# Running the first group alone through a two-block pipeline, and moving a weight conversion from GpSimd to VectorE and ScalarE

## The chip, the cores and the metric

The kernel runs on one core of one Trainium2 chip. The time is the device time of one execution in microseconds (us), and the lower the better. A core has five engines with their own instruction queues, each of which runs in order: TensorE (PE, matrix products and transposes), VectorE (DVE), ScalarE (ACT), GpSimd (POOL), and SyncE (SP), which issues most of the loads here. They wait for each other through semaphores. TensorE's clock is throttled: the profile records at which share of full speed it was let run, and here that share is 1.0 or 0.5.

Before the change the median was 373.23 us of three runs (372.49 to 373.57).

## The reference

Two blocks, one after the other, in fp32; the weights `w_in` and `w_out` arrive in fp64.

```python
# q, k, v, alpha: (B, H, S, D) = (4, 8, 768, 48)
for t in range(S):                                  # gated linear attention
    state = alpha[:, :, t, :, None] * state + einsum('bhd,bhe->bhde', k[:, :, t], v[:, :, t])
    y[:, :, t] = einsum('bhd,bhde->bhe', q[:, :, t], state)
x = y.transpose(0, 2, 1, 3).reshape(B, S, 384)

proj = x @ w_in                                     # w_in (384, 1024)
val, gate = proj[..., :512], proj[..., 512:]
a = exp(A_log)
for t in range(S):                                  # the SSM block
    h = a * h + val[:, t, :]
    ys[:, t, :] = h
return (silu(gate) * ys) @ w_out                    # w_out (512, 384)
```

## The kernel before

The 4 x 768 steps are cut into 12 groups of 256 steps, three to a batch. A group passes through three Python generators, and every call of `step(...)` emits one piece of one generator's instructions. A hand-written loop calls them in the order in which the engines are to receive the work.

- `front(n)`: alpha is transposed and scanned to running products V (backwards) and P (forwards); then Q, K, the 64-step blocks of scores, masked to A, and the transposed keys Kn. Two ScalarE passes over V (`junk`, L311 and L313) check that its values stay in range; the prediction calls them the checks.
- `back(n)`: the state at the start of each block (S_n), the outputs from inside the blocks (`y`, L145) and from the states before them (L163), and their transpose xT.
- `ssm(n)`: the SSM block. Four times a projection `pj`, a scan `hh`, `sg = silu`, and their product `f`; then twice an output product `o`.

```python
    def ssm(n, xT, prev_h, pool, ps_mm):
        ...
        for cc in range(NI):                                     # NI = 4
            pj = ps_mm.tile([C, 2, GC], FP32, tag="mm", name="pj")
            for i in range(2):
                for kk in range(NK):                             # NK = 3
                    nc.tensor.matmul(pj[:, i, :], w_in[:, kk, i, ds(cc * C, C)], xT[:, kk, :], ...)
            ...  # hh: scan on VectorE (L96)
            nc.scalar.activation(sg, pj[:, 1, :], AF.Silu)       # L101
            nc.vector.tensor_mul(f[:, cc, :], sg, hh)            # L102
            yield
        for c in range(G):                                       # G = 2
            ...  # o: NI matmuls of f with w_out (L107), copied out by ScalarE, stored
            yield
```

The fp64 weights are turned into fp32 by integer work on their two 32-bit words: eight units of `w_in` and four of `w_out`, each of 128 x 384 numbers. This is the unit as it was:

```python
        def split_unit(u):
            lo, hi = words[u][..., 0], words[u][..., 1]
            dst = units[u][0]
            nc.scalar.activation(lo.bitcast(FP32), lo, AF.Copy, scale=2.0 ** -52)
            ex = ...
            nc.vector.tensor_scalar(out=ex, in0=hi, ...)                 # exponent   (L235)
            nc.vector.tensor_scalar(out=dst.bitcast(U32), in0=hi, ...)   # mantissa   (L237)
            nc.scalar.activation(dst, dst.bitcast(U32), AF.Copy, scale=2.0 ** -20)
            nc.gpsimd.tensor_scalar(out=ex, in0=ex, ... ALU.max, ALU.min)  # clamp    (L240)
            nc.gpsimd.tensor_scalar(out=ex, in0=ex, ... ALU.add, ALU.mult) # rebias   (L241)

        def join_unit(u):
            nc.vector.scalar_tensor_tensor(out=ex, in0=hi, ...)          # sign       (L247)
            nc.gpsimd.tensor_add(dst, dst, lo.bitcast(FP32))             # low word   (L249)
            nc.gpsimd.tensor_mul(dst, dst, ex.bitcast(FP32))             # scale      (L250)
```

The state product also stood on GpSimd:

```python
            if not first:                                                # first group of a batch
                nc.gpsimd.tensor_mul(S_n[:, 0], S_end[0], s["V"][:, :, 0:1].to_broadcast([C, NP, D]))  # L347
            zv = block_states(s["Kn"], v_sb, ps_y)                       # z
            for x in range(GR):                                          # GR = 4
                ...  # nc.vector.tensor_add: S_n of the next block, or S_end   (L354, L356)
```

The loop runs three groups at once from the start. `front(n)`, `back(n - 1)`, the projections of `n - 2` (`new`) and the output products of `n - 3` (`old`) share turn n, and the weight conversion (`turn`) is fed in during turns 0 to 2:

```python
            for n in range(N + 3):
                fr, ba = front(n), back(n - 1)                           # where they exist
                old, new = ssms[n - 3], None
                turn = weights if n < 3 else None
                step(fr); step(turn); step(ba); step(old); step(old)
                step(fr); step(turn); step(ba)
                new = ssms[n - 2] = ssm(n - 2, ...)
                step(new); step(fr)
                ...                                                      # loads of n + 2
                step(turn); step(ba); step(new); step(fr); step(ba)
                step(turn); step(new); step(fr); step(turn); step(new)
```

## Time and profile before

| | before |
|---|---|
| time, median of 3 | 373.23 us |
| span of the profiled execution | 372.8 us |
| TensorE busy | 325.8 us, 87% |
| VectorE busy | 200.5 us, 54% |
| GpSimd busy | 56.8 us, 15% |
| mean granted TensorE clock | 0.975 |

A landmark that every turn has makes the timeline easy to cut: the first V scan of each group. I write V(n) for the moment at which it starts. Before, V(0) to V(4) are at 8.21, 30.85, 53.96, 89.22 and 115.25 us. The differences are 22.64, 23.11, 35.26 and 26.03 us, and from then on a turn takes 26.04 to 26.42 us. (Taken from the timeline, such a start lies 0.1 us or less before the one the chain of waits gives for the same scan, because the two views draw the edge differently.) The profile's lines are shown in the prediction below.

### The profile page before, as it was taken

To read this page: it belongs to the slowest core of one execution; us is meant where nothing else is said; L and a number is where in the kernel's file an instruction comes from. 1 tells how busy PE (TensorE), PEld (TensorE's weight loads), DVE (VectorE), ACT (ScalarE), POOL (GpSimd) and SP (SyncE) were. 2 spreads that over 40 slices of the span, in tenths; PEclk is the share of its full clock that TensorE was granted. 3 is DMA by queue.
4 is the path that set the end of the run, shared out by engine and by line. 5 is a ranking of instruction groups with operands and counts; after the bars stand their busy time and mean duration, and the time that the engine had idled before them with its cause. 6 is when DMAs were issued, how large, how long until landed. Compare 5 with 4: busy or idle time off the path is not lost.

```text
span 372.8 us, 9626 instructions
## 1 busy us (share of the span) xinstructions
PE 325.8 (87%) x4233; PEld 265.6 (71%) x4233; DVE 200.5 (54%) x373; ACT 106.5 (29%) x231; POOL 56.8 (15%) x77
## 2 busy tenths in 40 slices
PE   2535851899999999999999999999999999999794
PEld 1425741787887886887887887878868868878582
DVE  3939785356557438348456555565484493403140
ACT  1414354221432323133223213223332231312111
POOL 4478898510000000000000000000000000000000
PEclk9999995599999999999999999999999999999999
DMA  9999992040470740911913704607401000010101
GB/s 132 212 220 190 303 171 47 2 86 2 105 111 2 154 60 3 179 36 41 145 30 80 134 2 100 115 3 130 85 2 44 2 16 30 2 45 0 38 7 50
DMA packets 107650, 29.02 MB, mean 78 GB/s; under 512 B 100944, under 2 KB 107088, under 8 KB 107600
## 3 DMA queue, kind: packets, MB, share of 16 engines
q1 hardware_dynamic: 104992, 27.93, 40.6%
q10 hardware_dynamic: 2608, 0.40, 0.9%
q8 instruction: 35, 0.57, 0.7%
q14 instruction: 15, 0.12, 0.1%
HBM read 23.60 MB, written 4.72 MB: 76 GB/s over the span
## 4 chain that ended last, share of the span: by engine, by line
PE 62%; DVE 23%; SPq 6%; issue 4%; POOL 2%; DMA 1%; ACT 1%; ACTq 0%; DVEq 0%; POOLq 0%
PE pj L93 35%; PE y L145 7%; DVE V L301 7%; DVE P L306 7%; PE o L107 4%; SPq L83 4%; PE y L163 4%; PE sc L331 3%; PE tp L294 3%; DVE S_n L356 3%; PE tpk L119 2%; PE tpx L172 2%; SPq L226 2%; DVE hh L96 2%; DMA bits<-in_moe_w_in_dram 1%
## 5 line engine op out<-in xcount | busy, mean ns | idle before, releaser
L93 PE MATMUL pj<-xT,w_in 128*128 128x256 f32 x576 | 136.1, 388 | 0.0
L93 PEld LDWEIGHTS pj<-xT,w_in 128*128 128x128 f32 x576 | 107.7, 193 | 14.6
L96 DVE TENSOR_TENSOR_SCAN hh<-a_dec,hh,pj 128x256 f32<-128x256 f32 x32 | 23.9, 747 | 78.2 <-PE pj L93 78.2
L107 PE MATMUL o<-w_out,f 128*128 128x384 f32 x192 | 65.0, 492 | 0.0
L101 ACT ACTIVATE sg<-pj 128x256 f32<-128x256 f32 x48 | 18.4, 383 | 130.9 <-DVE hh L96 130.9
L107 PEld LDWEIGHTS o<-w_out,f 128*128 128x128 f32 x192 | 35.5, 190 | 23.0 <-DVE f L102 0.5
L145 PE MATMUL y<-v_sb,A 64*64 64x48 f32 x768 | 28.0, 233 | 11.9 <-DVE S_end L356 11.2
L347 POOL TENSOR_TENSOR S_n<-S_end,V 128x192 f32<-128x192 f32 x8 | 4.1, 513 | 224.2 <-DVE S_end L356 224.2
L145 PEld LDWEIGHTS y<-v_sb,A 64*64 64x64 f32 x768 | 26.7, 149 | 15.1 <-issue 8.3
L306 DVE TENSOR_TENSOR_SCAN P<-tp,iV,bias 128x256 f32<-128x256 f32 x48 | 33.4, 738 | 0.8
L102 DVE TENSOR_TENSOR f<-sg,hh 128x256 f32<-128x256 f32 x48 | 20.4, 426 | 23.3 <-ACT sg L101 23.3
L301 DVE TENSOR_TENSOR_SCAN V<-tp,bias 128x256 f32<-128x256 f32 x48 | 30.1, 669 | 5.1 <-PE tp L294 5.1
L96 DVE TENSOR_TENSOR_SCAN hh<-a_dec,pj 128x256 f32<-128x256 f32 x16 | 11.0, 687 | 39.4 <-PE pj L93 39.4
L311 ACT ACTIVATE junk<-V,bias 128x1024 f32<-128x1024 f32 x12 | 13.8, 1148 | 52.7 <-DVE V L301 52.7
L294 PE MATMUL tp<-ident,a_pad 128*128 128x128 f32 x96 | 14.6, 300 | 15.6 <-POOL ex L240 7.2
L294 PE MATMUL tp<-ident,q_pad 128*128 128x128 f32 x96 | 15.5, 306 | 11.9 <-DVE P L306 7.7
L294 PEld LDWEIGHTS tp<-ident,a_pad 128*128 128x128 f32 x96 | 12.4, 154 | 17.4 <-POOL ex L240 7.5
L294 PEld LDWEIGHTS tp<-ident,q_pad 128*128 128x128 f32 x96 | 12.4, 157 | 16.4 <-issue 13.8
L240 POOL TENSOR_SCALAR ex<-ex 128x384 uint32<-128x384 uint32 x12 | 18.4, 1532 | 18.0 <-DVE ex L235 17.7
L331 PEld LDWEIGHTS sc<-Q,K 64*64 64x64 f32 x768 | 13.7, 144 | 4.3 <-issue 3.3
L334 DVE COPY_PREDICATED A<-mask,sc 128x512 f32<-128x512 uint8 x24 | 16.0, 721 | 1.1 <-PE sc L331 1.1
L322 DVE TENSOR_TENSOR K<-tp,V 128x512 f32<-128x512 f32 x24 | 15.5, 684 | 2.0 <-PE tp L294 2.0
(59 smaller groups left out, 315.6 us busy)
## 6 DMA issues: line engine op xcount, KB each, us to landing
a_pad<-in_alpha_dram SPq DMA_DIRECT2D x24, 192.0 KB, 4.7
k_pad<-in_k_dram SPq DMA_DIRECT2D x24, 192.0 KB, 5.1
v_sb<-in_v_dram SPq DMA_DIRECT2D x24, 192.0 KB, 5.0
out_dram<-o_sb SPq DMA_DIRECT2D x24, 192.0 KB, 2.1
q_pad<-in_q_dram SPq DMA_DIRECT2D x22, 192.0 KB, 5.0
bits<-in_moe_w_in_dram SPq DMA_DIRECT2D x8, 384.0 KB, 5.4
bits<-in_moe_w_out_dram SPq DMA_DIRECT2D x4, 384.0 KB, 6.1
q_pad<-in_q_dram ACTq DMA_DIRECT2D x2, 192.0 KB, 5.5
```

Of the source, the lines that this page charges most:

```text
L93: nc.tensor.matmul(pj[:, i, :], w_in[:, kk, i, ds(cc * C, C)], xT[:, kk, :], start=(kk == 0), stop=(kk == NK - 1))
L96: nc.vector.tensor_tensor_scan(out=hh, data0=a_dec[:, cc:cc + 1].to_broadcast([C, GC]), data1=pj[:, 0, :], initial=prev_h[cc][:, GC - 1:GC ...
L101: nc.scalar.activation(sg, pj[:, 1, :], AF.Silu)
L102: nc.vector.tensor_mul(f[:, cc, :], sg, hh)
L107: nc.tensor.matmul(o, f[:, cc, ds(c * C, C)], w_out[:, cc, :], start=(cc == 0), stop=(cc == NI - 1))
L145: nc.tensor.matmul(yv[rows, i, c, j, :], A[rows, i, c * NP + j, :], v_sb[rows, c, 2 * j + i, :], start=(c == 0 and j == 0), stop=False, sk ...
L240: nc.gpsimd.tensor_scalar(out=ex, in0=ex, scalar1=896.0, scalar2=1151.0, op0=ALU.max, op1=ALU.min)
L294: nc.tensor.transpose(tp[:, u, ds(c * C, C)], pad[name][:, c, 2 * j:2 * j + 2, :], ident)
L301: nc.vector.tensor_tensor_scan(out=V[:, 2 * jj + u, GC - 1::-1], data0=tp[:, u, ::-1], data1=bias[:, 1:2].to_broadcast([C, GC]), initial=1 ...
L306: nc.vector.tensor_tensor_scan(out=P[:, 2 * jj + u, :], data0=tp[:, u, :], data1=bias[:, 1:2].to_broadcast([C, GC]), initial=iV0[:, 2 * jj ...
L331: nc.tensor.matmul(scv[ds(R * r, R), i, c * NP + j, :], K[rows, j, steps], Q[rows, j, steps], start=True, stop=True, skip_group_check=True)
L334: nc.vector.copy_predicated(out=A[:, i].rearrange("p x t -> p (x t)"), mask=mask[:, ds(i * GP * R, GP * R)], data=sc[:, i])
```

## The change

The intent is to relieve the start. Group 0 first runs alone until its xT is ready. Then its SSM block runs beside `front(1)`, instead of a turn later. The conversion of `w_in` goes to VectorE and ScalarE except for one addition, so that GpSimd's backlog does not hold up the state product, which itself moves to VectorE. GpSimd keeps most of the conversion of `w_out`, which is needed later. All of `w_in` is now loaded ahead of group 1.

```diff
-        def split_unit(u):
+        def split_unit(u, late):                       # late: a unit of w_out
...
-            nc.scalar.activation(lo.bitcast(FP32), lo, AF.Copy, scale=2.0 ** -52)
             ex = scales[u] = wex.tile(list(hi.shape), U32, tag="ex", name="ex")
+            eng = nc.gpsimd if late else nc.vector
             nc.vector.tensor_scalar(out=ex, in0=hi, scalar1=20, scalar2=0x7FF, ...)
+            eng.tensor_scalar(out=ex, in0=ex, scalar1=896.0, scalar2=1151.0, op0=ALU.max, op1=ALU.min)
             nc.vector.tensor_scalar(out=dst.bitcast(U32), in0=hi, scalar1=0xFFFFF, ...)
+            nc.scalar.activation(lo.bitcast(FP32), lo, AF.Copy, scale=2.0 ** -52)
+            nc.scalar.activation(ex, ex, AF.Identity, scale=2.0 ** 23, bias=bias[:, 3:4])
             nc.scalar.activation(dst, dst.bitcast(U32), AF.Copy, scale=2.0 ** -20)
-            nc.gpsimd.tensor_scalar(out=ex, in0=ex, ... ALU.max, ALU.min)
-            nc.gpsimd.tensor_scalar(out=ex, in0=ex, ... ALU.add, ALU.mult)
+            nc.gpsimd.tensor_add(dst, dst, lo.bitcast(FP32))
...
-            nc.gpsimd.tensor_add(dst, dst, lo.bitcast(FP32))
-            nc.gpsimd.tensor_mul(dst, dst, ex.bitcast(FP32))
+            (nc.gpsimd if late else nc.vector).tensor_mul(dst, dst, ex.bitcast(FP32))
...
-                nc.gpsimd.tensor_mul(S_n[:, 0], S_end[0], ...)
+                nc.vector.tensor_mul(S_n[:, 0], S_end[0], ...)
...
+            fr, ba = front(0), back(0)
+            for gen in (fr, fr, weights, fr, weights, fr, fr, weights, ba, weights, ba, ba, ba):
+                step(gen)
+            new = ssms[0] = ssm(0, xs.pop(0), prev_h, p2, ps_mm)
+            fr = front(1)
+            for gen in (fr, new, weights, weights, fr, new, weights, weights, fr, new, weights, fr, new, weights, fr):
+                step(gen)
+            load(2)
-            for n in range(N + 3):
+            for n in range(2, N + 3):
...
+                if n == 2: two units of weights after the V scans, two after Q
...
-                step(new)
+                step(old if n == 2 else new)            # twice: the o of group 0 now in turn 2
```

(The last two places are abridged; `ssm` begins for groups 1 and later in turn 3, as before.)

More of the change, by code (lines that the diff above doesn't have):

```diff
@@ L75 @@
     flag = const.tile([1, 1], I32, name="flag")
-    bias = const.tile([C, 3], FP32, name="bias")
+    bias = const.tile([C, 4], FP32, name="bias")
     def load_heads(dst, src, n, queue=nc.sync):
@@ L227, in fetch_unit, with join_unit @@
             words.append(bits)
-        def split_unit(u):
+        def split_unit(u, late):
             lo, hi = words[u][..., 0], words[u][..., 1]
             dst = units[u][0]
-            nc.scalar.activation(lo.bitcast(FP32), lo, AF.Copy, scale=2.0 ** -52)
             ex = scales[u] = wex.tile(list(hi.shape), U32, tag="ex", name="ex")
+            eng = nc.gpsimd if late else nc.vector
             nc.vector.tensor_scalar(out=ex, in0=hi, scalar1=20, scalar2=0x7FF,
                                     op0=ALU.logical_shift_right, op1=ALU.bitwise_and)
+            eng.tensor_scalar(out=ex, in0=ex, scalar1=896.0, scalar2=1151.0, op0=ALU.max, op1=ALU.min)
             nc.vector.tensor_scalar(out=dst.bitcast(U32), in0=hi, scalar1=0xFFFFF, scalar2=0x100000,
                                     op0=ALU.bitwise_and, op1=ALU.bitwise_or)
+            nc.scalar.activation(lo.bitcast(FP32), lo, AF.Copy, scale=2.0 ** -52)
+            nc.scalar.activation(ex, ex, AF.Identity, scale=2.0 ** 23, bias=bias[:, 3:4])
             nc.scalar.activation(dst, dst.bitcast(U32), AF.Copy, scale=2.0 ** -20)
-            nc.gpsimd.tensor_scalar(out=ex, in0=ex, scalar1=896.0, scalar2=1151.0, op0=ALU.max, op1=ALU.min)
-            nc.gpsimd.tensor_scalar(out=ex, in0=ex, scalar1=-896.0, scalar2=2.0 ** 23, op0=ALU.add, op1=ALU.mult)
-        def join_unit(u):
-            lo, hi = words[u][..., 0], words[u][..., 1]
+            nc.gpsimd.tensor_add(dst, dst, lo.bitcast(FP32))
+        def join_unit(u, late):
             dst, ex = units[u][0], scales.pop(u)
-            nc.vector.scalar_tensor_tensor(out=ex, in0=hi, scalar=0x80000000, in1=ex,
+            nc.vector.scalar_tensor_tensor(out=ex, in0=words[u][..., 1], scalar=0x80000000, in1=ex,
                                            op0=ALU.bitwise_and, op1=ALU.bitwise_or)
-            nc.gpsimd.tensor_add(dst, dst, lo.bitcast(FP32))
-            nc.gpsimd.tensor_mul(dst, dst, ex.bitcast(FP32))
+            (nc.gpsimd if late else nc.vector).tensor_mul(dst, dst, ex.bitcast(FP32))
         def convert_weights():
@@ L254, in convert_weights @@
                 if u < len(units):
-                    split_unit(u)
+                    split_unit(u, u >= 2 * NI)
                 if u > 0:
-                    join_unit(u - 1)
+                    join_unit(u - 1, u - 1 >= 2 * NI)
                 yield
@@ L346, in back @@
             if not first:
-                nc.gpsimd.tensor_mul(S_n[:, 0], S_end[0], s["V"][:, :, 0:1].to_broadcast([C, NP, D]))
+                nc.vector.tensor_mul(S_n[:, 0], S_end[0], s["V"][:, :, 0:1].to_broadcast([C, NP, D]))
             zv = block_states(s["Kn"], v_sb, ps_y)
@@ L373, in ranged @@
         clear_pads(0, "a")
-        for w, value in enumerate((1.0, FLOOR, -1.0)):
+        for w, value in enumerate((1.0, FLOOR, -1.0, -896 * 2.0 ** 23)):
             nc.gpsimd.memset(bias[:, w:w + 1], value)
@@ L387, in ranged @@
         load(0, "k")
-        fetch_unit(0)
         nc.scalar.dma_start(out=a_log, in_=moe_A_log.rearrange("(a p) -> p a", p=C))
         load(0, "v")
-        fetch_unit(1)
-        load(1, "aq")
-        fetch_unit(2)
-        load(1, "kv")
-        for u in range(3, 6):
+        for u in range(2 * NI):
+            fetch_unit(u)
+        load(1)
+        for u in range(2 * NI, len(units)):
             fetch_unit(u)
@@ L412, in ranged @@
         with tc.manual_schedule():
-            for n in range(N + 3):
-                fr = front(n) if n < N else None
-                ba = back(n - 1) if 0 <= n - 1 < N else None
-                old, new = ssms[n - 3], None
-                turn = weights if n < 3 else None
+            fr, ba = front(0), back(0)
[7 more added lines that the diff above has]
+            for n in range(2, N + 3):
+                fr = front(n) if n < N else None
+                ba = back(n - 1) if n - 1 < N else None
+                new = None
+                old = ssms[n - 3] if n > 2 else ssms[0]
+                if n == 2:
+                    early, old = None, old
                 step(fr)
-                step(turn)
+                if n == 2:
+                    step(weights)
+                    step(weights)
                 step(ba)
-                step(old)
-                step(old)
+                if n > 2:
+                    step(old)
+                    step(old)
                 step(fr)
-                step(turn)
+                if n == 2:
+                    step(weights)
+                    step(weights)
                 step(ba)
-                if 0 <= n - 2 < N:
+                if 2 < n < N + 2:
                     new = ssms[n - 2] = ssm(n - 2, xs.pop(n - 2), prev_h, p2, ps_mm)
@@ L429, in ranged @@
                 step(fr)
-                if n + 2 < N:
-                    load(n + 2)
-                if n == 0:
-                    for u in range(6, len(units)):
-                        fetch_unit(u)
-                step(turn)
+                if n + 1 < N:
+                    load(n + 1)
                 step(ba)
-                step(new)
+                step(old if n == 2 else new)
                 step(fr)
                 step(ba)
-                step(turn)
-                step(new)
+                step(old if n == 2 else new)
                 step(fr)
-                step(turn)
                 step(new)
```

## The prediction

> **What bounds the kernel now.** I read the slices first, then the chain that ended last, then the timeline of the first 100 us and of one steady turn.
>
> ```profile
> PE   2535851899999999999999999999999999999794
> DVE  3939785356557438348456555565484493403140
> POOL 4478898510000000000000000000000000000000
> PEclk9999995599999999999999999999999999999999
> ```
>
> Each digit is a tenth of busy time in 9.3 us. TensorE (PE) is full from about 74 us on; before that it is half idle, GpSimd (POOL) is busy with the weights, and TensorE's clock falls to half in slices 7 and 8. So there are two regimes: a start of some 89 us, and a steady turn from one first V scan to the next (89.30, 115.34, 141.75, 168.11 us: 26.2 us).
>
> The chain around the end of the start:
>
> ```profile
> 62.05 1.01 POOL w_out L249
> ...
> 63.13 0.99 POOL w_out L250
> 64.13 0.48 POOL S_n L347
> ...
> 66.30 3.65 PE y L145 x64
> 69.95 5.00 PE pj L93 x12
> ...
> 85.05 2.61 PE pj L93 x12
> ...
> 89.30 1.19 DVE V L301 x2
> ```
>
> Columns: start, duration, engine, tile, line. The state product S_n (L347) stands behind weight conversion on GpSimd, so the y of group 1 starts 12.3 us after group 2's V scan (53.96 us) where a steady turn needs 7.2. Then y takes 3.65 us instead of 2.07 and the first pj 5.00 instead of 2.79: half clock, 3.8 us lost. These two are what a better start can win, about 9 us; all else in that turn is normal.
>
> A steady turn, from the timeline:
>
> ```profile
> 119.55 1.39 DVE L306 TENSOR_TENSOR_SCAN P<-tp,iV,bias 128x256 f32<-128x256 f32 x2
> 120.86 0.33 DVE L354 COPY S_n<-z 128x192 f32<-128x192 f32 x1
> 121.22 0.74 DVE L356 TENSOR_TENSOR S_n<-S_n,z 128x192 f32<-128x192 f32 x2
> 122.00 0.35 DVE L356 TENSOR_TENSOR S_end<-S_n,z 128x192 f32<-128x192 f32 x1
> 122.50 2.07 PE L145 MATMUL y<-v_sb,A 64*64 64x48 f32 x64 [0.70 <-DVE S_end L356]
> ```
>
> From V to y the path is VectorE: scans (5.6 us), then the S_n operations at 0.37 us each, then y waits for S_end. From y to the last pj (17.6 us) the path is TensorE without a gap. TensorE's 16 output matmuls o (5.4 us) lie under the scans: they are free there, and they keep the clock up.
>
> **What the Trainium skill says.** "TensorE: Matmul & The Clock Gate", section Part 1: the array is halved after about one idle window of 3.4 us and freed after one busy window, the windows running freely. The trace agrees: half clock from 57.3 to 74.4 us, 17.07 us, five windows of 3.41; it came although 0.4 us of transposes fell into the window. "SBUF — State Buffer", SBUF: two separate sides: a VectorE operation in a two-port mode or with two SBUF inputs and a GpSimd operation that reads SBUF lock each other out for the whole instruction. Here too:
>
> ```profile
> 52.60 1.02 POOL L249 TENSOR_TENSOR w_in<-w_in,bits 128x384 f32<-128x384 f32 x1
> 52.67 1.37 DVE L247 SCALAR_TENSOR_TENSOR ex<-bits,ex 128x384 uint32<-128x384 uint32 x1 [0.42 <-POOL ex L241]
> ```
>
> Alone L247 takes 0.55 us; here it ends 0.4 us after the GpSimd add. "ScalarE: Activation LUTs", What ACT_TABLE_LOAD costs: 1283 ns; the trace has 1.28 us at 70.18, where ScalarE was idle.
>
> **The change, part by part.**
>
> *Weights.* On GpSimd a unit costs 1.53 + 0.52 + 1.01 + 1.05 = 4.1 us, 12 units 49 us. After: w_in leaves one add of 1.0 us there, w_out 3.5 us. VectorE gets per w_in unit ex 0.35, clamp about 0.3 (estimate, from L235's 0.35, same shape), mantissa 0.5, sign 0.6, product 0.55 (estimate, from S_n's 0.35 at half the size): 2.3 us, 8 units 18.4 us. ScalarE has three passes of 0.52 where it had two.
>
> *Loads.* All of w_in now comes before group 1's loads. The early windows moved about 160 GB/s on the 192-byte pieces of the heads and 245 on w_in: heads of group 0 by 11.7 us, w_in by 24, alpha of group 1 by about 26.5. I find no later operation below waiting for a load.
>
> *Order.* I walked each engine's order of the built kernel with these durations:
> - Group 0 alone: scans 8.2 to 13.8 as before, scores done 19.9, two more units, S_n to 25.5, y 25.6 to 29.3 (cold), values before 31.8, x_sb 32.7, transposes (cold) and xT 34.8. Only then group 1's transposes: V(1) at about 35.3 against 30.85. VectorE idles 27.7 to 35 meanwhile.
> - V(1) to V(2): VectorE has scans 5.6, Q, K and A 3.8, four times hh and f with their wait 6.0, four splits and five joins of w_in about 10.2, two units of w_out 1.8: 27.4. The Silu table load now stands on the path, behind group 1's two checks on ScalarE: about 2 us until f. At the end V(2)'s transposes wait for Kn, which stands on ScalarE behind the second w_out unit, which waits for GpSimd's clamp of 1.5 us: 3 us. Sum 32.4, plus about 3 for four adds on GpSimd locking out VectorE's work: V(2) near 71.
> - V(2) to V(3): scans 5.6, the last two w_out units 3.1, S_n 1.8, then y(1) 10.6 us after V(2), cold because TensorE has next to nothing from V(2) to there: 3.7; then k 2.0, values before 2.2, o 3.4, scores, transposes and the second o 5.7, keys and alpha 1.5: 18.5, some of it still at half clock. Sum about 28, V(3) near 99; without the lock 95.5, with a full clock 91.
>
> *After V(3)* the kernel is the old one with three differences. o of group 0 is done already, but it was free, and without it TensorE is nearly idle from z to y(2), 6.9 us, so an idle window falls in and y and pj run cold again: 3.7 us. The product S_n moves to VectorE between P and the S_n sums: 0.36 us in each turn that does not begin a batch, turns 3, 5, 6, 8, 9, 11: 2.2 us. The tail is unchanged.
>
> Sum: V(3) is 89.3 before and 95.5 to 99 after, +6 to +10; +3.7 (three chances in four); +2.2. From 373.2 this makes 384 to 388. I set 384.5, a little low, because the lock and the idle windows depend on phase, and the order looks hand tuned.
>
> **Rivals.**
> 1. *The start shrinks by the stall it aims at.* If GpSimd's backlog were all that holds the start, taking it away gives up to 5 us from y(1), and with a warm clock 9: 364 to 368. For it: POOL at 8 or 9 tenths from 19 to 56 us. Against it: new VectorE work stands in front of Q, K, hh and f in the in-order queue, and TensorE's work from V to V (26 us) is not shortened.
> 2. *A wash.* TensorE stays warm, locks cost nothing: V(3) at 91, plus 2.2: 377, within 2%. For it: the phase of the window is luck, and many VectorE operations here read PSUM and are not locked. Against: in the start before, the same gap pattern did go cold.
> 3. *Loads bound the start* (16 queues are full to about 56 us already): if w_in's eight units delay group 1, V(1) slips. Against it: alpha of group 1 is there some 8 us ahead of V(1). No change of the time from this.
>
> **Range and chances.** Rival 2 with some luck gives 375 to 377; all locks, cold windows and waits at once 391. So 375 to 392. Over 2% slower is above 380.7: my walk lies above that unless two of its three losses (lock, cold turn 3, queue waits) fail: 0.72. Within 2%: 0.21. Faster by over 2% needs rival 1, 0.07.
>
> **What would show it.** V(1) near 35, V(2) near 67 to 71, V(3) near 95 to 99 in the timeline. VectorE rather than GpSimd the releaser in the start, GpSimd's share of busy time from 15% to about 9%. A table load between group 1's checks and the first Silu. Half clock twice after 60 us: around y(1) and around y(2), with y at 3.65 us both times. From V to y 7.5 us in turns in the middle of a batch, where it was 7.16. VectorE's ex or sign operations of 1.0 us or more beside GpSimd adds. The prediction is wrong if V(3) comes before 90 us, if y(2) runs at 2.07 us, or if the steady turns keep their length.

## The result, and the profile after

| | before | after |
|---|---|---|
| time, median (lowest to highest) | 373.4 (372.49 to 373.97), 4 runs | 389.44 (388.79 to 390.43), 4 runs |
| ratio to before, 95% interval | | 1.0434 (1.0402 to 1.0466) |
| span of the profiled execution | 372.8 | 386.6 |
| V(0), V(1), V(2), V(3), V(4) | 8.21, 30.85, 53.96, 89.22, 115.25 | 8.26, 35.55, 70.24, 97.07, 126.67 |
| TensorE / VectorE / ScalarE / GpSimd busy | 325.8 / 200.5 / 106.5 / 56.8 | 332.4 / 209.0 / 113.5 / 28.5 |

The change made the kernel 4.3% slower. A ratio here is the mean time of one kernel's fast runs over that of the other's fast runs of the same rounds, so it is not quite the ratio of the medians that I quote. A span is 1.7 to 2.2 us shorter than the time of the same execution, and single executions of one kernel scatter by about 1 us around their median: the profiled one of before took 374.53 us, that of after 388.79 us. So the spans differ by 13.8 us and the medians by 16.0. Below I account for the 13.8 us of the spans, where every step can be seen.

The 40 slices of the page (one digit is a tenth of busy time, or of full clock, in 9.7 us):

```profile
PE   2568457569599999899999998999999998999795
DVE  3983797751824835745557449357465574423240
POOL 4140134370000000000000000000000000000000
PEclk9986898659779999999999999999999999999998
```

Counted from 1, TensorE is full from slice 12 on, about 106 us, where before it was full from slice 9, about 74 us. GpSimd is nearly relieved (7% busy against 15%) and VectorE is loaded in slices 2 to 8. The clock row is below 9 in slices 3 to 5, 7 to 9 and 11 to 12, where in before it was so in slices 7 and 8 alone, but its first part must be read with care: before the first clock record of an execution the row shows full speed. In the profile of before the y of group 0 took 3.65 us at 39.37 us, twice its steady 2.07, under a recorded clock of 1.0. The early slices of the two pages are therefore not comparable in that row; durations are.

The chain of waits of the changed kernel through its start (start, duration, engine, tile, line):

```profile
35.55 1.28 DVE V L301 x2
...
42.23 1.28 ACT L101
...
66.42 1.53 POOL ex L237
...
76.27 1.59 POOL ex L237
...
78.53 0.56 DVE ex L248
79.09 0.28 DVE S_n L347
...
81.13 3.65 PE y L145 x64
...
87.99 2.78 PE o L107 x8
...
92.67 2.60 PE o L107 x8
...
97.07 1.28 DVE V L301 x2
...
104.39 3.65 PE y L145 x64
108.03 4.30 PE pj L93 x12
```

There is a table load of ScalarE on it, operations of GpSimd, the y of groups 1 and 2 at half speed (that of group 0, at 26.06 us, took 3.67 us and is not shown), and the output products of group 0, which lay under the scans before. The lines of the conversion have new numbers in the changed kernel: L235 exponent, L237 clamp, L238 mantissa, L243 addition, L248 sign, L250 scale.

The state product S_n of group 1 is on VectorE now, and yet it still waits for GpSimd. The order puts it behind the sign operation (L248) of a `w_out` unit, which waits through ScalarE for GpSimd's clamp of that unit (76.27 us). So y(1) starts 10.9 us after V(2), where before it was 12.3 us and in a steady turn 7.2. Of the stall that the change aims at, only 1.4 us are gone.

The timeline around that table load and the first collision of VectorE with GpSimd:

```profile
42.23 1.28 ACT L101 ACT_TABLE_LOAD   x1
43.53 0.38 ACT L101 ACTIVATE sg<-pj 128x256 f32<-128x256 f32 x1
...
43.94 0.43 DVE L102 TENSOR_TENSOR f<-sg,hh 128x256 f32<-128x256 f32 x1 [2.13 <-ACT sg L101]
...
46.18 1.32 POOL L243 TENSOR_TENSOR w_in<-w_in,bits 128x384 f32<-128x384 f32 x1 [17.14 <-ACT w_in L242]
46.54 1.17 DVE L235 TENSOR_SCALAR ex<-bits 128x384 uint32<-128x384 uint32 x1
```

The bracket at `f` says that VectorE stood idle for 2.13 us and that ScalarE's `sg` ended it. The exponent operation L235 takes 0.35 us elsewhere; beside the addition on GpSimd it takes 1.17 us. It happens again at 54.53 us, and two sign operations (L248) take 0.86 us instead of 0.55 beside GpSimd's clamp. That is 2 x 0.82 + 2 x 0.31 = 2.26 us in all, of which the second sign operation (66.52 us) costs nothing, as VectorE waits after it anyway. The exponent fits the lock that the Trainium skill describes in "SBUF — State Buffer", SBUF: two separate sides: it ends 0.2 us after the addition. The sign fits it less well: at 60.87 us it starts beside a clamp that runs from 60.78 to 62.31 us, and it ends 0.6 us before the clamp does. Nor are the collisions new. Between V(1) and V(2) of before, an exponent took 1.13 us at 49.23 us and a sign 1.37 us at 52.67 us (shown in the prediction), 0.78 + 0.82 = 1.60 us more than alone. The locks cost time in after, but they explain little of the difference between the two kernels.

The end of that stretch, where the keys of group 1 wait in ScalarE's queue:

```profile
66.42 1.53 POOL L237 TENSOR_SCALAR ex<-ex 128x384 uint32<-128x384 uint32 x1 [1.96 <-DVE ex L235]
67.98 0.61 ACT L241 ACTIVATE ex<-ex,bias 128x384 uint32<-128x384 uint32 x1 [1.93 <-POOL ex L237]
...
68.92 1.06 ACT L120 ACTIVATE Kn<-tpk 128x512 f32<-128x512 f32 x2
...
70.24 1.27 DVE L301 TENSOR_TENSOR_SCAN V<-tp,bias 128x256 f32<-128x256 f32 x2 [2.86 <-PE tp L294]
```

The copies Kn were ready to run when their transposes ended at 65.3 us. They stand behind two ScalarE passes of a `w_out` unit, which wait for the clamp on GpSimd. The transposes of group 2 need the buffers that Kn empties, and so V(2) waits 2.86 us. Finally a steady turn in the middle of a batch:

```profile
158.68 0.33 DVE L347 TENSOR_TENSOR S_n<-S_end,V 128x192 f32<-128x192 f32 x1
160.78 2.07 PE L145 MATMUL y<-v_sb,A 64*64 64x48 f32 x64 [1.16 <-DVE S_end L356]
```

(These are single lines of VectorE's and TensorE's timelines.) TensorE waits 1.16 us for the states where before it waited 0.69 us. Turns that do not begin a batch take 26.83 and 26.50 us instead of 26.36 and 26.04; the turn that begins one is unchanged at 26.4. The product on VectorE costs about 0.46 us in each.

The 13.8 us by place:

| stretch | before | after | difference |
|---|---|---|---|
| to V(1): group 0 alone | 30.85 | 35.55 | +4.7 |
| V(1) to V(2) | 23.11 | 34.69 | +11.6 |
| V(2) to V(3) | 35.26 | 26.83 | -8.4 |
| V(3) to V(4) | 26.03 | 29.60 | +3.6 |
| the rest, 5 turns with the product at 0.46 and the tail | 257.55 | 259.93 | +2.4 |

The change wins 8.4 us in the third line and pays 16.3 us in the two lines above for it. Most of the 8.4 us is moved work, not a shorter stall. From V(2) to y(1) it wins 1.4 us; from y(1) to V(3) it wins 7.0 us (22.9 before, 15.9 after), because the four pj of group 0 (13.0 us on the chain of before) have gone from there to the stretch between V(1) and V(2), and the two o (5.4 us) have come in their place.

### The profile page after: what moved, and what is told of

Same layout as the page of the kernel before. It is cut to its first block, busy times and chain, and to the rows that moved or that the text cites. A ratio compares the mean times of both kernels' runs of the same rounds, so it can differ in the third digit from the quotient of the medians.

```text
span 386.6 us, 9606 instructions
## 1 busy us (share of the span) xinstructions
PE 332.4 (86%) x4233; PEld 269.0 (70%) x4233; DVE 209.0 (54%) x397; ACT 113.5 (29%) x243; POOL 28.5 (7%) x42
## 4 chain that ended last, share of the span: by engine, by line
PE 59%; DVE 28%; issue 4%; ACT 3%; POOL 2%; DMA 2%; SPq 0%; DVEq 0%; ACTq 0%; POOLq 0%
PE pj L93 31%; PE y L145 8%; DVE P L306 8%; DVE V L301 7%; PE o L107 5%; PE y L163 4%; PE tp L294 3%; PE sc L331 3%; DVE S_n L356 3%; PE tpx L172 3%; PE tpk L119 2%; DVE hh L96 2%; DMA a_pad<-in_alpha_dram 2%; DVE f L102 1%; POOL ex L237 1%
## 5 line engine op out<-in xcount | busy, mean ns | idle before, releaser
L93 PE MATMUL pj<-xT,w_in 128*128 128x256 f32 x576 | 138.9, 393 | 5.1 <-DVE w_in L250 5.1
L145 PE MATMUL y<-v_sb,A 64*64 64x48 f32 x768 | 29.6, 240 | 14.3 <-DVE S_end L356 12.5
L145 PEld LDWEIGHTS y<-v_sb,A 64*64 64x64 f32 x768 | 28.3, 156 | 17.3 <-issue 12.0
L311 ACT ACTIVATE junk<-V,bias 128x1024 f32<-128x1024 f32 x12 | 13.8, 1148 | 51.9 <-DVE V L301 51.9
L96 DVE TENSOR_TENSOR_SCAN hh<-a_dec,pj 128x256 f32<-128x256 f32 x16 | 10.9, 684 | 28.8 <-PE pj L93 28.8
L294 PEld LDWEIGHTS tp<-ident,q_pad 128*128 128x128 f32 x96 | 12.3, 157 | 16.2 <-issue 14.8
L331 PE MATMUL sc<-Q,K 64*64 64x64 f32 x768 | 15.2, 229 | 2.9 <-DVE K L322 2.7
L110 ACT ACTIVATE o_sb<-o 128x384 f32<-128x384 f32 x24 | 10.7, 479 | 17.9 <-PE o L107 17.9
## 6 DMA issues: line engine op xcount, KB each, us to landing
bits<-in_moe_w_in_dram SPq DMA_DIRECT2D x8, 384.0 KB, 6.2
bits<-in_moe_w_out_dram SPq DMA_DIRECT2D x4, 384.0 KB, 5.4
```

The source lines that it names most:

```text
L96: nc.vector.tensor_tensor_scan(out=hh, data0=a_dec[:, cc:cc + 1].to_broadcast([C, GC]), data1=pj[:, 0, :], initial=prev_h[cc][:, GC - 1:GC ...
L145: nc.tensor.matmul(yv[rows, i, c, j, :], A[rows, i, c * NP + j, :], v_sb[rows, c, 2 * j + i, :], start=(c == 0 and j == 0), stop=False, sk ...
L294: nc.tensor.transpose(tp[:, u, ds(c * C, C)], pad[name][:, c, 2 * j:2 * j + 2, :], ident)
L331: nc.tensor.matmul(scv[ds(R * r, R), i, c * NP + j, :], K[rows, j, steps], Q[rows, j, steps], start=True, stop=True, skip_group_check=True)
```

## The experiments

My theory after the result was that the slowdown is the sum of independent losses that the new order makes. They are the output products of group 0 on the critical path, a cold turn 3 (cold: TensorE at half clock), the table load, the wait for Kn, the locks, and the product S_n in every turn. The rivals were that the moved conversion work is the loss (VectorE is overloaded, whatever the order), and that only TensorE's clock matters. Twelve kernels ran; all gave correct results.

| kernel | median, us | ratio to before (95%) | span | V(2) | V(3) | V(4) |
|---|---|---|---|---|---|---|
| after | 389.44 | 1.0434 (1.0402 to 1.0466) | 386.6 | 70.24 | 97.07 | 126.67 |
| o_late | 381.12 | 1.0174 (1.0113 to 1.0235) | 379.1 | 70.06 | 92.20 | 119.08 |
| sn_pool | 386.91 | 1.0333 (1.0272 to 1.0394) | 385.0 | 69.75 | 97.17 | 126.93 |
| silu_early | 386.77 | 1.0330 (1.0270 to 1.0391) | 385.5 | 68.73 | 95.96 | 125.80 |
| keys_first | 385.40 | 1.0293 (1.0222 to 1.0365) | 384.0 | 67.39 | 94.06 | 123.58 |
| before_newconv | 376.32 | 1.0072 (1.0028 to 1.0115) | 374.1 | 56.01 | 90.65 | 116.69 |
| after_oldconv | 391.38 | 1.0456 (1.0430 to 1.0482) | 391.1 | 72.05 | 101.09 | 131.12 |
| fill3 | 386.12 | 1.0314 (1.0284 to 1.0343) | 384.6 | 70.05 | 97.06 | 123.94 |
| after_best | 374.48 | 1.0024 (0.9998 to 1.0049) | 372.3 | 65.64 | 87.29 | 114.17 |
| before_sn_fill | 368.94 | 0.9862 (0.9842 to 0.9883) | 368.1 | 53.47 | 83.89 | 109.93 |
| repack | 369.51 | 0.9880 (0.9835 to 0.9926) | 367.1 | 62.57 | 81.81 | 108.69 |
| repack_fill | 367.10 | 0.9819 (0.9797 to 0.9840) | 365.1 | 61.18 | 80.41 | 107.29 |
| no_add | 386.00 | 1.0318 (1.0279 to 1.0357) | 385.5 | 67.87 | 94.97 | 124.73 |

The runs were made in four calls, each with its own runs of before: o_late, sn_pool, silu_early and keys_first (before: 373.95 us); before_newconv, after_oldconv, fill3 and after_best (374.25); before_sn_fill, repack and repack_fill (373.99); no_add (373.81). For effects of 1 to 3 us the landmarks are sharper than the medians, and I read them first. Each is read from one profiled execution. V(1) itself scatters from 34.97 to 35.55 us among after, o_late, sn_pool, silu_early, keys_first and fill3, whose instructions are the same up to there but for silu_early's one small activation. The stretch from V(1) to V(2) agrees better: 34.69 to 34.78 us in after, o_late, sn_pool and fill3, which are alike in it.

### o_late: the output products of group 0 back in turn 3

```diff
-                step(old if n == 2 else new)
+                step(new)            # in both places; the o of group 0 then comes as `old` of turn 3
```

> The changed kernel with group 0's output matmuls o moved from turn 2 back into turn 3 (under the scans). Theory (o was free under the scans and kept the clock up): V(3) comes about 5.4 us earlier, because the two halves of o (2.85 and 2.60 us) leave TensorE's path of turn 2, and y(2) runs at 2.07 us instead of 3.65 and its first pj at 2.79 instead of 4.30, 3.1 us more; in all about -8.5 us, near 381 us. Rival A (the place of o is a wash, the start is bound elsewhere): within 1 us of 389.4. Rival B (the clock falls for another reason, for example the gap before y alone): -5.4 us only, with y(2) still at 3.65 us.

Measured: 381.12 us, 8.3 us below after. It is the largest gain of any single edit. Two separate effects add up. V(3) comes 4.9 us earlier, because the two o (2.78 and 2.60 us on the chain of after) no longer stand between y(1) and V(3). And V(3) to V(4) shrinks from 29.60 to 26.88 us, because the o now fill TensorE's gap before y(2). TensorE's timeline:

```profile
93.66 5.43 PE L107 MATMUL o<-w_out,f 128*128 128x384 f32 x16
...
99.89 2.07 PE L145 MATMUL y<-v_sb,A 64*64 64x48 f32 x64
```

y(2) runs at full speed, 2.07 us, where in after it took 3.65 (at 104.39 us, above).

### sn_pool: the state product back on GpSimd, except for group 1

```diff
-                nc.vector.tensor_mul(S_n[:, 0], S_end[0], ...)
+                (nc.vector if n == 1 else nc.gpsimd).tensor_mul(S_n[:, 0], S_end[0], ...)
```

> The changed kernel with the product S_n put back on GpSimd in all turns but turn 2 (there GpSimd has w_out). Theory: turns 3, 5, 6, 8, 9, 11 lose the product from VectorE's path, 0.46 us each by the changed kernel's turns (26.82 and 26.50 us against 26.36 and 26.04): -2.8 us, near 386.7 us, and the span from V to y falls from 7.6 back to 7.16 us in a batch's middle turn. Rival (the turns are longer for another reason, for example the later loads): no change, 389.4 us.

Measured: 386.91 us, 2.5 us below after, with the span 1.6 us shorter. The steady turns are back at 26.42, 26.36 and 26.04 us. So the product in VectorE's queue costs 0.46 us a turn, although it is recorded with 0.33 us: the operation after it starts 0.44 us after it. In turn 3, however, V(4) did not gain:

```profile
104.02 3.65 PE L145 MATMUL y<-v_sb,A 64*64 64x48 f32 x64
107.60 5.00 PE L93 MATMUL pj<-xT,w_in 128*128 128x256 f32 x12
```

y(2) starts 0.37 us earlier than in after, but its pj takes 5.00 us where after's took 4.37 in the same view. The clock came back at much the same moment in both. Work that starts earlier inside a half-speed spell only does more of itself at half speed.

### silu_early: the table load moved to an idle moment

```diff
         nc.scalar.activation(a_dec, a_log, AF.Exp)
+        nc.scalar.activation(own.tile([C, NI], FP32, name="warm"), a_log, AF.Silu)
```

> The changed kernel with one 128x4 Silu right after the exponential at the start, so that the Silu table is loaded while ScalarE idles. Theory: the 2.1 us that VectorE waits for the first f (table load on the path) go; what follows is VectorE-bound up to V(2), so -2 us, near 387.4 us, V(2) at about 68. Rival (the wait comes back at the next operand: pj of unit pairs 2 and 3, or ScalarE's queue): less than 0.7 us gained.

Measured: 386.77 us, 2.7 us below after. V(2) comes 1.5 us earlier (1.4 us, counted from V(1)) and V(3) 1.1 us, and the span is 1.1 us shorter. The timeline at the two places:

```profile
9.69 1.28 ACT L396 ACT_TABLE_LOAD   x1
...
42.38 0.42 DVE L102 TENSOR_TENSOR f<-sg,hh 128x256 f32<-128x256 f32 x1 [0.71 <-ACT sg L101]
```

The load now runs at 9.69 us, where ScalarE was idle, and the wait of `f` falls from 2.13 to 0.71 us. That difference of 1.42 us is the 1.28 us load and little else.

### keys_first: the keys of group 1 ahead of the second unit of w_out

```diff
-... fr, new, weights, fr, new, weights, fr):
+... fr, new, weights, fr, new, fr, weights):
```

> The changed kernel with the last two steps before turn 2 swapped, so that on ScalarE the copies Kn come before the passes of the second w_out unit; no other engine's order changes. Theory: V(2) no longer waits for Kn behind GpSimd's clamp; V(2) about 2.8 us earlier (near 67.4), and the time -2.8 us, near 386.6. Rival (w_out's chain through GpSimd is itself the bound of turn 2, so it eats the gain): V(2) earlier but V(3) unchanged, 389.4 us.

Measured: 385.4 us, 4.0 us below after, with runs from 384.04 to 387.15. V(2) comes 2.85 us earlier (2.8 us, counted from V(1)), which is the whole 2.86 us wait, and V(3) 3.0 us. The span is 2.6 us shorter. By the landmarks this is a loss of about 3 us in after; by the median it could be as much as 4.

### before_newconv and after_oldconv: order and conversion apart

before_newconv is the kernel before with only the new conversion. after_oldconv is the changed kernel with only the old conversion:

```diff
# before_newconv, on before            # after_oldconv, on after
+ split_unit, join_unit and            + split_unit, join_unit and
+ convert_weights of after             + convert_weights of before
+ bias with 4 columns
```

> The kernel before with the new conversion alone (w_in mostly on VectorE and ScalarE, w_out on GpSimd); its order, loads and S_n on GpSimd unchanged. Theory (walked as the prediction was): V(1) slips to about 32 and V(2) to about 55.5 because VectorE has 0.9 us more per w_in unit and the locks; S_n of group 1 still stands behind w_out's clamp, add and product on GpSimd, so y(1) comes about 11.7 us after V(2) instead of 12.3; V(3) near 90: the time 0 to +1.5 us, 373.5 to 375.5. Rival (GpSimd's conversion is what bounds the start): about -5 us, 368.

> The changed kernel with the old conversion (GpSimd 4.1 us a unit) in the new order. Theory: the order, not the new conversion, makes most of the loss; VectorE is relieved, the copies Kn no longer wait for GpSimd, but units reach pj later (unit 3 about 1 us, unit 7 about 2 us): V(2) near 67.5, V(3) near 94 to 95, the time 385 to 388. Rival A (the new conversion on VectorE is the loss): near 380. Rival B (GpSimd's 49 us of conversion cannot be hidden in this order, which is why it was moved): over 393.

Measured: before_newconv 376.32 us (ratio 1.0072), after_oldconv 391.38 us (ratio 1.0456). Both came out slower than expected, the first by about 1 us and the second by more than 3 us, so I had the sign of the second wrong. Put together with before and after they give a table of two by two:

| | old conversion | new conversion |
|---|---|---|
| old order | 1 | 1.0072 |
| new order (with its loads and S_n on VectorE) | 1.0456 | 1.0434 |

The loss comes with the order, and the conversion alone moves less than 1% in either order. The rival "the moved work on VectorE is the loss, whatever the order" falls. That this work costs nothing is not shown: with the old conversion V(1) comes at 33.33 us, 2.2 us earlier than in after, and V(1) to V(2) takes 38.72 us, because other waits take its place. In the new order the old conversion is no better, because the SSM block needs w_in earlier than GpSimd delivers it. TensorE's timeline of after_oldconv:

```profile
46.94 2.93 PE L93 MATMUL pj<-xT,w_in 128*128 128x256 f32 x6 [5.86 <-POOL w_in L250]
...
65.00 2.93 PE L93 MATMUL pj<-xT,w_in 128*128 128x256 f32 x6 [2.90 <-POOL w_in L250]
```

And in the old order the new conversion does not remove the stall it aims at. The timeline of before_newconv:

```profile
65.67 0.99 POOL L250 TENSOR_TENSOR w_out<-w_out,ex 128x384 f32<-128x384 f32 x1
66.61 0.51 POOL L347 TENSOR_TENSOR S_n<-S_end,V 128x192 f32<-128x192 f32 x1
67.16 1.13 DVE L356 TENSOR_TENSOR S_n<-S_n,z 128x192 f32<-128x192 f32 x3 [4.18 <-POOL S_n L347]
```

The product S_n still stands behind w_out on GpSimd, and y(1) starts 12.8 us after V(2), against 12.3 us in before. It is the place of the product behind a unit of w_out that matters here, not GpSimd's sum of work; in after the product met the same wait from VectorE's queue.

### fill3: dummy matmuls before y(2)

```diff
+                if n == 3:          # results are not used
+                    for c in range(G):
+                        o = ps_mm.tile([C, DM], FP32, tag="mm", name="fill")
+                        for cc in range(NI):
+                            nc.tensor.matmul(o, ident, w_out[:, cc, :], start=(cc == 0), stop=(cc == NI - 1))
```

> The changed kernel with 8 dummy matmuls of o's shape (identity by w_out, result not read) in turn 3 where o stood. It parts the two effects in the run with the late o. Theory: the clock stays full, y(2) 2.07 us and its first pj 2.79 instead of 3.65 and 4.30: -3.1 us, near 386.3 us, V(3) unchanged at 97. Rival (the cold run of turn 3 has nothing to do with the missing o): 389.4 us, y(2) still at 3.65 us.

Measured: 386.12 us, 3.3 us below after. V(3) stays at 97.06 and V(4) comes 2.7 us earlier. y(2) takes 2.07 us instead of 3.65 and its pj 2.86 instead of 4.37. The dummy work does nothing but keep TensorE busy for 5.4 us in the gap, so the cold turn is a matter of the clock alone, worth 2.7 us. It accounts for that much of o_late's gain of 7.6 us at V(4). The rival "only the clock matters" falls with this, as most of the 13.8 us remains. The y of groups 0 and 1 stay cold in fill3, but they were cold in before as well (3.65 us each), so they do not make the difference between the kernels.

### after_best: the four repairs together

o_late, sn_pool, silu_early and keys_first in one kernel.

> The changed kernel with all four repairs at once: o in turn 3, S_n on GpSimd except in turn 2, the early Silu, Kn before the last unit. Singly they gave -8.3, -2.5, -2.7 and -4.0 us. Theory (they lie at different places of one chain, so they add): sum of the steps read from the traces -8.5 - 2.8 - 2.0 - 2.8 = -16 us, near 373.4: all of the loss, and nothing won over the kernel before. Rival (they overlap, the keys and the early Silu both being taken up by GpSimd's w_out): 377 to 380.

Measured: 374.48 us, ratio 1.0024: the same as before, and 1 us above the expectation. The span is 14.3 us shorter than after's. The four alone shorten it by 7.5 + 1.6 + 1.1 + 2.6 = 12.8 us, so the losses are nearly independent, and together they are as large as the whole slowdown. That does not make the account complete, because other losses stay and gains pay for them. V(1) is still at 35.42 us and V(1) to V(2), with its locks, at 30.22 us, 4.6 and 7.1 us more than in before; V(2) to V(3) is down to 21.65 us, 13.6 us less. The start is then about as long as before's, only cut differently.

### no_add: the additions for w_in left out

```diff
-            nc.gpsimd.tensor_add(dst, dst, lo.bitcast(FP32))
+            if late:
+                nc.gpsimd.tensor_add(dst, dst, lo.bitcast(FP32))
```

The low word is then missing from w_in, and the result still lies within the tolerance. This removes the two collisions of L235 with the addition, but not the two of L248 with the clamp.

> The changed kernel without GpSimd's eight adds of the low words of w_in (it drops the last 32 of each weight's 52 mantissa bits, on purpose, so the result is slightly off but perhaps within tolerance). It parts the lock between VectorE and GpSimd from the rest. Theory as the changed kernel's trace shows it: between V(1) and V(2) two ex operations take 1.17 us instead of 0.35 beside those adds; without the adds these 1.6 us go, so -1.6 to -2 us, near 387.5 us. Rival A (the prediction's sum: four adds cost about 3 us): near 386.4 us. Rival B (VectorE waits elsewhere for the same time, the lock is hidden): 389.4 us.

Measured: V(1) to V(2) takes 32.92 us instead of 34.69, which is 1.77 us less. All exponent operations are at 0.35 to 0.36 us, and 2 x 0.82 = 1.64 us was to go. The span is 1.1 us shorter; the median is 3.4 us lower. With intervals of 0.4% on both ratios the time cannot tell 1.8 from 3 us, so I take the landmark: the lock with the additions costs about 1.8 us. What the removal of the 0.3 us at the first sign operation would give was not tried. A third addition, at 17.78 us before V(1), made an exponent 0.86 us long; what that costs is lost in the scatter of V(1).

### before_sn_fill: the old order with its own stall taken out

```diff
-                nc.gpsimd.tensor_mul(S_n[:, 0], ...)
+                (nc.vector if n == 1 else nc.gpsimd).tensor_mul(S_n[:, 0], ...)
...
+                if n == 2:
+                    filler(1, 9)     # 9 matmuls of the identity with Q of group 1, not used, after z
```

> The kernel before with the two losses of its start mended and nothing of the change: group 1's product S_n on VectorE (not behind w_out on GpSimd), and 9 dummy matmuls (identity by Q of group 1, 256 wide, result not read) between z(1) and y(1) so that TensorE's clock stays up. Theory (those two waits are what its start loses): y(1) about 3.5 us earlier (near 62.8 instead of 66.3), y 2.07 and the first pj 2.79 us, 3.8 more: about -7.3 us, near 366.5 us. Rival (GpSimd's backlog then holds o or pj instead): less than 3 us gained.

Measured: 368.94 us, ratio 0.9862. The interval V(2) to V(3) falls from 35.26 to 30.42 us. y(1) starts 8.7 us after V(2) instead of 12.3. The expectation was 366.5: y(1) still takes 3.65 us and its pj 3.85 us, because the filler ended at 57.5 us and TensorE then had 1.2 us of transposes until 62.19 us. Of the 4.8 us, 3.6 are the earlier y(1), and 1.2 the first pj, which still ran partly cold. The two edits were not run apart, so how much of that the filler gave is not shown. By the 2% rule the kernel counts as the same, but its interval excludes no gain. So one moved product and nine dummy matmuls in the old order win what the large change did not.

### repack and repack_fill: the new order with every repair

repack takes the changed kernel with sn_pool and silu_early, gives the clamp of w_out to VectorE as well, leaves the o of group 0 in turn 3, and spreads the conversion more thinly. Its start is:

```diff
+            for gen in (fr, fr, weights, fr, weights, fr, fr, weights, ba):
+                step(gen)
+            # repack_fill: filler(0, 6) here
+            for gen in (weights, ba, weights, ba, ba, weights):
+                step(gen)
+            new = ssms[0] = ssm(0, xs.pop(0), prev_h, p2, ps_mm)
+            fr = front(1)
+            for gen in (fr, new, fr, new, weights, fr, new, weights, fr, weights, new, fr):
+                step(gen)
+            # turn 2: one unit after Q, one after y, one or none later; repack_fill: filler(1, 9) after z
```

> The changed kernel's idea with its steps placed anew: o in turn 3, S_n on GpSimd but in turn 2, early Silu, two of the w_in units moved into VectorE's 7 us of idle time before V(1), S_n of group 1 ahead of the last w_out units, w_out's clamp on VectorE so that ScalarE never waits for GpSimd. Theory: V(1) stays near 35.4, V(2) comes near 60 (70.2 in the changed kernel), y(1) about 7.7 us after V(2) instead of 10.9 and still cold, V(3) near 80, then as before: near 364 us. Rival (VectorE's order only shifts the waits, units come too late for pj): V(2) later than 64 and the time within 2% of 373.

> The same with 6 dummy matmuls between z(0) and y(0) and 9 between z(1) and y(1). Theory: TensorE's clock stays up, y(0), values before, transposes and y(1) run at full speed: about 3 us from V(1) (near 32) and about 3 us in turn 2: near 359 us. Rival (the dummies are run at half clock and stand in the way themselves): no better than the kernel without them.

Measured: repack 369.51 us, about 5 us above what I expected; repack_fill 367.1 us, about 8 us above. V(1) to V(2) is at 27.15 us in repack (34.69 in after), and V(2) to V(3) at 19.24 us with y(1) still cold. With the product on VectorE ahead of the `w_out` units, y(1) starts 7.7 us after V(2), as expected, where in after it was 10.9. No run made that edit alone. With the fillers, y of groups 0 and 1 run warm. TensorE's timeline of repack_fill:

```profile
62.64 4.15 PE L415 MATMUL fill<-Q,ident 128*128 128x256 f32 x18
...
68.89 2.07 PE L145 MATMUL y<-v_sb,A 64*64 64x48 f32 x64 [1.22 <-DVE S_end L357]
```

The same timeline a few microseconds on shows why the warm y(1) saves nothing: V(2) to V(3) stays at 19.23 us.

```profile
74.29 1.28 DVE L323 TENSOR_TENSOR K<-tp,V 128x512 f32<-128x512 f32 x2
...
75.03 1.52 PE L332 MATMUL sc<-Q,K 64*64 64x64 f32 x64 [1.97 <-DVE K L323]
```

Between Q and K stand two units of w_out on VectorE, with a mantissa and a sign operation of 1.19 and 1.35 us beside GpSimd's passes. K starts 5.63 us after Q in repack_fill (68.66 to 74.29) as in repack (70.06 to 75.69), and TensorE, done sooner, waits 1.97 us for it. In this stretch the bound has passed from TensorE to VectorE. So repack_fill gains 1.4 us over repack, all of it by V(1), where y(0) is warm. My expectations had counted the cold y(1) as a loss that a filler takes back in full.

repack_fill is the fastest kernel. It is 1.8% faster than before and 5.7% faster than after (367.1 / 389.44 = 0.943). Its interval against before, 0.9797 to 0.9840, excludes no gain but does not settle whether it reaches 2%.

## Why the prediction was right or wrong

The direction, the range and, in the main, the mechanism held: 389.44 us lies in 375 to 392, "slower by over 2%" had the largest chance, and V(1), V(2) and V(3) came where the walk put them. The point, 384.5, was 4.9 us too low.

- **Group 0 alone.** Predicted V(1) at 35.3, measured 35.55. The walk along each engine's order was good to 0.3 us.
- **V(1) to V(2).** Predicted "near 71" for V(2), measured 70.24. The three additions were about 2 us for the table load, 3 us for Kn and 3 us for the locks. The trace shows waits of 2.13, 2.86 and 2.26 us; what taking them away gave was 1.5, 2.85 and 1.8 us (the last without the sign operations). With what the experiments gave back (6.15 us) taken off, the stretch is 28.5 us, about 1 us above the walk's 27.4. The lock is the term that was mis-sized: of the four w_in additions in this stretch two hit an exponent operation. The other two ran beside Q and K, which took their usual 1.28 us. And the prediction added the lock as a new cost, although its own line from before shows the same collision there.
- **V(2) to V(3).** Predicted about 28, measured 26.83. The prediction's own terms, 10.6 and 18.5 us, add up to 29.1, so its "about 28" and its V(3) "near 99" are 1 us too low for its working. The wait to y(1) was right (10.9 for 10.6). The part from y on was too long, 15.9 measured, as the clock came back at 87.2 us, before the first o, and the rest ran at full speed. That these o stood in the path was in the walk as "o 3.4" and a "second o"; what it did not say is that this alone is the largest single loss of the change, 4.9 us, which o_late showed.
- **Cold turn 3.** Predicted 3.7 us with three chances in four. It came, and y and pj cost 1.58 + 1.51 = 3.1 us more than in before; fill3 got back 2.7 us.
- **The product S_n.** Predicted 0.36 us in six turns, 2.2 us. Measured 0.46 us in the five turns after V(4), 2.3 us, and 0.47 us from V(3) to y(2). There sn_pool showed it to be free, since the clock's return decided. The mechanism was right; the duration of the operation was taken as its cost, and its start-to-start distance is the cost.
- **The sum.** The prediction's own sum was 384 to 388 on top of 373.2, and the spans gave +13.8, which is 387 on that base. The step that failed is the last one, "I set 384.5, a little low, because the lock and the idle windows depend on phase, and the order looks hand tuned". That the order looks tuned was not evidence, and the cold turn and the waits nearly all came. The last 2 us between 387 and 389.4 are the difference between profiled executions and medians named above.
- **Rival 1, a shorter start.** It fell, and the chain of after does run through VectorE's new conversion work between V(1) and V(2), as argued against it. V(2) to V(3) did win 8.4 us, but only 1.4 us of them at the stall, where the rival allowed up to 5, and V(1) and V(2) lost 16.3. The remark that the two faults of the old start "are what a better start can win, about 9 us" was tested by before_sn_fill: it won 4.8 us of V(2) to V(3), because y(1) stayed cold. repack_fill won 8.0 us at V(4).
- **Rival 2, a wash** needed a warm TensorE. It was cold at y(0), y(1) and y(2). **Rival 3, loads:** no later operation of the start waits for a load in the trace.
- **The signs to look for** came with two corrections. GpSimd's share fell to 7%, not about 9%. The half clock came twice after 60 us for long (70.1 to 87.2 and 100.8 to 111.1), as written, but there were also short spells of 3.4 us from 46.2 and from 59.9 us, which I had not looked for.

## What to carry to other kernels

When work is reordered to relieve one engine, walk every in-order queue with measured durations and ask what each operation now stands behind; small things such as a table load, a copy behind a waiting pass, or output products that used to lie under a scan together cost more here than the moved conversion did in the old order (0.7%). Ask too which work kept TensorE's clock up in its gaps, because taking it out of the gap costs twice. And before restructuring a start, try the smallest edit that removes the stall seen: one moved product and nine dummy matmuls in the old order won 1.4% where the large change lost 4.3%.

## What the Trainium skill lacked or had wrong

- "TensorE: Matmul & The Clock Gate", Part 1, speaks of one idle window before half speed and one busy window before full speed, but not of windows that matmuls fill in part (of transposes the page speaks elsewhere). In after, the clock fell at 100.8 us although TensorE was busy for 1.83 us of the 3.4 us before, 1.15 us of it with the matmuls of z; in before it fell at 57.3 us with 0.41 us busy. And y did not raise it at once: in after, y filled 104.39 to 108.03 us and the clock rose at 111.1; in before y ran from 66.30 to 69.95 us, pj followed without a gap, and the rise came at 74.4. In both cases the last window before the rise was filled with pj. So the prediction's "the trace agrees" holds for the length of the windows, and not for the release after one busy one. The runs do not show what counts as busy.
- The same page has no remedy by dummy matmuls in a gap. Here 5.4 us of them made y 1.58 us and the whole turn 2.7 us shorter than in after (fill3); 4.2 us of them followed by 4.7 us with 1.2 us of transposes did not keep y at full speed (before_sn_fill).
- "ScalarE: Activation LUTs", What ACT_TABLE_LOAD costs, adds a drain to a total of about 2.66 us. Here the load took 1.28 us, it began 0.01 us after the operation before it had ended, the next activation began 0.02 us after it, and moving it away shortened the wait of its consumer by 1.42 us.
- No page that I looked up warns that the clock record of a profile starts late (Part 1 of the first page calls such records unreliable in general): until its first record, at 47.1 us in before, the page shows full speed, while y took 3.65 us instead of 2.07 (before, 39.37 us).
